# Off-by-one softmax attention and a squared-relu MLP on one core: relus and a copy moved to ScalarE, first-product steps moved between units, the last tile in two pieces

## The chip, the cores and the metric

The kernel runs on one core of one Trainium2 chip. A core has TensorE (PE, matrix products), VectorE (DVE), ScalarE (ACT), GpSimd (POOL) and SyncE (SP), each of which takes its instructions in order and waits for the others by semaphores. The metric is the device time of one execution in microseconds, as the median of several runs. The kernel before takes 412.63 us (three runs, 412.62 to 412.65).

## The reference

```python
batch, n_heads, seq, head_dim = (8, 12, 448, 64)        # q, k, v: float32
scale = 1.0 / np.sqrt(q.shape[-1])
scores = scale * np.matmul(q, k.transpose(0, 1, 3, 2))
m = np.max(scores, axis=-1, keepdims=True)
e = np.exp(scores - m)
attn = e / (np.sum(e, axis=-1, keepdims=True) + np.exp(-m) + 1e-09)
attn_out = np.matmul(attn, v)
# ...
x = np.ascontiguousarray(attn_out.transpose(0, 2, 1, 3)).reshape(B * S, H * D)   # 3584 x 768
h = x @ w_in                                             # 768 x 2048
r = np.maximum(h, 0.0)
g = r * r
out = (g @ w_out).astype(np.float32)                     # 2048 x 768
```

With the maximum taken out, attention is exp(s) divided by (sum of exp(s) + 1). The product with `w_in` is called the first product here, the one with `w_out` the second.

## The kernel before

Attention works in units: one pair of heads for some queries of one batch. Units 0 to 5 are the six pairs of batch 0 for its first 192 queries, units 6 to 11 the same pairs for the other 256, units 12 to 17 the pairs of batch 1 with all 448. From unit 18 on three units are taken together. A unit's scores come in two halves (`scores(u, et, 0)` and `scores(u, et, 1)`, here the first and second scores), each followed by exp on ScalarE. VectorE then adds the exps up (`add_chunks`), TensorE makes row sums from that with a matrix of ones, ScalarE makes the reciprocal by ln and exp, and VectorE normalises.

Beside the attention, the first product of the tokens already attended runs in small steps, to fill TensorE: `drain(ns)` takes steps from the queue `ins` until they have used up `ns`, and stops, also inside a tile. A tile of the first product covers two blocks of 128 hidden units in batch 0, has 12 steps there, and ends with relu and multiply. What is emitted where in these loops is also the order in which each engine gets it. Tiles in PSUM (`mp`, three buffers, before unit 18) are shared by the first product, the transposes and the row sums.

```python
    def transposes(b, pr):
        tp = mp_tile(FP16)
        for i, name in enumerate("qk"):
            for s in range(RUN):
                for h in range(2):
                    nc.tensor.transpose(tp[64 * h:64 * h + 64, i, P * s:P * s + P],
                                        naturals[name, b, pr][:, h, s, :], ident[0:P, 0:P])
        if b not in qks:
            qks[b] = qk_pool.tile([128, 3, COLS], FP16, name="qk")
        parts = (0, S // 2, S) if b == 0 and pr < 3 else (0, S)
        for x, y in zip(parts, parts[1:]):
            nc.vector.tensor_copy(qks[b][:, 0:2, pr * S + x:pr * S + y], tp[:, :, x:y])

    # ...
    def add_chunks(u, et, es, half, step):
        n = u[3]
        if n == S:
            e = et.rearrange("p (k x) -> p k x", k=RUN)
            if step < 2:
                nc.vector.tensor_add((es, half[:, 0:2 * S])[step], e[:, 2 * step], e[:, 2 * step + 1])
            else:
                nc.vector.tensor_add(es, es, half[:, 0:2 * S])
    # ...
    def row_sums(us, sums):

        n = us[0][3]
        m = n * len(us)
        zp = mp_tile()
        for j, (u, parts) in enumerate(zip(us, sums)):
            for x, es in enumerate(parts):
                total = es[:, 0:2 * n]
                if n < S:
                    total = total.rearrange("p (h n) -> p h n", h=2)
                for h in range(2):
                    nc.tensor.matmul(zp[64 * h:64 * h + 64, j * n:(j + 1) * n], ones, of_head(total, u, h),
                                     start=(x == 0), stop=(x == len(parts) - 1))
        rcp = z_pool.tile([128, 512], FP32, name="rcp")
        nc.scalar.activation(out=rcp[:, 0:m], in_=zp[:, 0:m], func=AF.Ln, bias=one_b)
        nc.scalar.activation(out=rcp[:, 0:m], in_=rcp[:, 0:m], func=AF.Exp, scale=-1.0)
        return rcp
    # ...
    def mp_tile(dtype=FP32):
        if joined[0] >= 0:
            joined[0] += 1
        pool, name = (x_psum, "xp") if joined[0] > 0 and joined[0] % 4 == 0 else (m_psum, "mp")
        return pool.tile([128, 512] if dtype == FP32 else [128, 2, 512], dtype, name=name)

    # ...
    def product(out_, lhsT, rhs, start, stop):

        if mode[0] == COLS2:
            for x in (0, 64):
                nc.tensor.matmul(out_[x:x + 64], lhsT[:, x:x + 64], rhs, start=start, stop=stop)
        else:
            nc.tensor.matmul(out_, lhsT, rhs, start=start, stop=stop)

    def relu_squared(hp, t0, n, f0, per):
        m = per * n
        rt = r_pool.tile([128, 512], FP16, name="rt")
        nc.vector.tensor_scalar(out=rt[:, 0:m], in0=hp[:, 0:m], scalar1=0.0, scalar2=None, op0=ALU.max)
        r = rt[:, 0:m].rearrange("p (j n) -> p j n", j=per)
        nc.vector.tensor_mul(gs[:, f0:f0 + per, t0 % RING:t0 % RING + n], r, r)

    def tile_in(t0, n, f0, per):

        xt, x0 = xts[t0 // S], t0 % S
        hp = mp_tile()
        for j in range(per):
            fb = f0 + j
            for dc in range(DCH):
                product(hp[:, j * n:(j + 1) * n], win[:, dc, fb * 128:(fb + 1) * 128],
                        xt[:, dc, x0:x0 + n], start=(dc == 0), stop=(dc == DCH - 1))
                if j < per - 1 or dc < DCH - 1:
                    yield n / 2.4
        relu_squared(hp, t0, n, f0, per)
        yield n / 2.4
    # ...
    def store(c, ot, n0, n1):
        end = c + 128
        while c < end:
            b = c // S
            step = RUN if b in ON_PE else 2
            rows = out[b * S:(b + 1) * S, n0:n1].rearrange("(p t) m -> t p m", t=step)
            t, p = c % S // (S // step), c % S % (S // step)
            m = min(S // step - p, end - c)
            o = c + 128 - end
            nc.sync.dma_start(out=rows[t, p:p + m, :], in_=ot[o:o + m, n0:n1])
            c += m

    # ...
    # end of tile_out(tok, n0, w): the second product of 128 tokens and w columns
        else:
            nc.scalar.activation(out=ot[:, n0:n0 + w], in_=op[:, 0:w], func=AF.Copy, scale=OUT_SCALE)
        # ...
        last = tok + 128 == NT
        if n0 + w == DM or last:
            store(tok, ot, n0 if last else 0, n0 + w)
        yield w / 2.4
    # ...
    def queue(t0, n):

        per = max(1, 512 // n)
        first = 0
        if t0 + n == FIRST:
            first = 2 * per
            ns = first * DCH * n / 2.4
            ins.append([ns, ns, tiles_in_early(n, 0, per, DCH - 2)])
        for f0 in range(first, NFFB, per):
            ns = per * DCH * n / 2.4
            ins.append([ns, ns, tile_in(t0, n, f0, per)])

    def complete(upto):

        while groups[0] + 128 <= upto:
            last = groups[0] + 128 == NT
            for n0, w in ((0, HALF), (HALF, 256), (HALF + 256, 128)) if last else ((0, HALF), (HALF, HALF)):
                ns = NFFB * w / 2.4
                outs.append([ns, ns, tile_out(groups[0], n0, w)])
            groups[0] += 128

    def left():
        return sum(t[0] for t in ins)

    def one(tiles):

        got = next(tiles[0][2])
        tiles[0][0] -= got
        if tiles[0][0] < 1.0:
            tiles.pop(0)
        return got

    def drain(ns):
        while ins and ns > 0:
            ns -= one(ins)

    def run(tiles, n=1):
        for _ in range(min(n, len(tiles))):
            for _ in tiles.pop(0)[2]:
                pass
    # ...
    FIRST = 192
    units = [(0, pr, 0, FIRST) for pr in range(NPAIR)] + [(0, pr, FIRST, S - FIRST) for pr in range(NPAIR)]
    units += [(b, pr, 0, S) for b in range(1, B) for pr in range(NPAIR)]
    NU = len(units)

    transpose_at = {pr - 1: [(0, pr)] for pr in range(1, NPAIR)}
    for i, at in ((10, (1, 0)), (11, (1, 1)), (11, (1, 2)), (13, (1, 3)), (14, (1, 4)), (15, (1, 5)), (16, (2, 0)),
                  (17, (2, 1)), (17, (2, 2))):
        transpose_at.setdefault(i, []).append(at)

    # ...
    for i in range(NPAIR, 2 * NPAIR):
        u, et, es, half = begin(i)
        two = units[i - 2:i] if i % 2 == 0 else None
        if i % 2 or i == NPAIR:
            xp = x_psum.tile([128, 512], FP32, name="xp")
        mode[0] = COLS2
        scores(u, et, 0)
        if i == NPAIR:
            sums(i - 1)
            values_of(i - 2, xp)
            values_of(i - 1, xp)
            rcp = sums_of(i - 2)
            normalise(two, xp, rcp)
            scores(u, et, 1)
            queue(0, FIRST)
            share[0] = left() / (NPAIR + 4)
        else:
            for at in transpose_at.get(i, ()):
                transposes(*at)
            drain(16 * FIRST / 2.4 if i == NPAIR + 1 else share[0] * 0.45)
            scores(u, et, 1)
            values_of(i - 1, xp)
            if two:
                rcp = sums_of(i - 2)
            drain(share[0] * 0.3)
        add_chunks(u, et, es, half, 1)
        if two and i > NPAIR:
            normalise(two, xp, rcp)
        add_chunks(u, et, es, half, 2)
        if i > NPAIR:
            drain(share[0] * 0.25)
        if i == NPAIR + 5:
            load_natural(2, 0, 3)
            for n0 in (0, HALF):
                for j in range(2):
                    load_wout(n0, j, 2)


    for i in range(2 * NPAIR, 3 * NPAIR):
        u, et, es, half = begin(i)
        prev = units[i - 1]
        first = i == 2 * NPAIR
        if not first:
            xp = x_psum.tile([128, 512], FP32, name="xp")
        mode[0] = COLS2
        scores(u, et, 0)
        for at in transpose_at.get(i, ()):
            transposes(*at)
        if i == 2 * NPAIR + 3:
            load_natural(2, 3, 6)
            load_v(2, 0, 6)
            stage(3)
        drain(share[0] * (1.2 if first else 0.45))
        scores(u, et, 1)
        if first:
            done = units[i - 2:i]
            values(prev, ets.pop(i - 1), xp, prev[3])
            rcp = row_sums(done, (ess.pop(i - 2)[0:1], ess.pop(i - 1)[0:1]))
        else:
            done = [prev]
            rcp = row_sums(done, (ess.pop(i - 1)[0:1],))
            values(prev, ets.pop(i - 1), xp)
        drain(share[0] * 0.15)
        for step in range(3):
            add_chunks(u, et, es, half, step)
            drain(share[0] * (0.15, 0.1, 0.15)[step])
        if i == 3 * NPAIR - 1:
            run(ins, len(ins))
            rcps[i] = row_sums([u], (ess.pop(i)[0:1],))
        normalise(done, xp, rcp)
        if first:
            queue(FIRST, S - FIRST)
            share[0] = left() / (NPAIR - 0.2)
    # ... units 18 to 47, then the last tokens: mode FULL, run(ins), run(outs)
```

Of the kernel before, what the change touches and what calls it, by code (L numbers as in the profile page):

```python
# [10 lines left out]
AF = mybir.ActivationFunctionType  # L11
ALU = mybir.AluOpType
# [3 lines left out]
def kernel(  # L16
# [9 lines left out]
    nc = tc.nc  # L26

    B, H, S, D = q.shape
    NT, DM = out.shape
    DF = moe_w_in.shape[1]  # L30
    NPAIR = H // 2
    DCH = DM // 128
    NFFB = DF // 128
# [4 lines left out]
    HALF = DM // 2  # L38
# [36 lines left out]
    whole, vns, qks, xts, naturals, stages = {}, {}, {}, {}, {}, {}  # L75
# [77 lines left out]
# [8 lines that stand above are left out]
            qks[b] = qk_pool.tile([128, 3, COLS], FP16, name="qk")  # L161
        parts = (0, S // 2, S) if b == 0 and pr < 3 else (0, S)
        for x, y in zip(parts, parts[1:]):
            nc.vector.tensor_copy(qks[b][:, 0:2, pr * S + x:pr * S + y], tp[:, :, x:y])  # L164

# [64 lines left out]
    def values(u, et, xp, o=0):  # L232
        b, pr, _, n = u
        for kk in range(RUN):
            for h in range(2):
                nc.tensor.matmul(xp[64 * h:64 * h + 64, o:o + n], vns[b][:, 2 * pr + h, kk, :],  # L236
                                 of_head(chunk(et, u, kk // 2, kk), u, h), start=(kk == 0), stop=(kk == RUN - 1))
# [18 lines that stand above are left out]
# [21 lines left out]

    FULL, COLS2, ROWS2 = range(3)
    mode = [FULL]
    ots = {}  # L280

    def product(out_, lhsT, rhs, start, stop):
# [7 lines left out]
    def relu_squared(hp, t0, n, f0, per):  # L290
        m = per * n
        rt = r_pool.tile([128, 512], FP16, name="rt")
        nc.vector.tensor_scalar(out=rt[:, 0:m], in0=hp[:, 0:m], scalar1=0.0, scalar2=None, op0=ALU.max)  # L293
        r = rt[:, 0:m].rearrange("p (j n) -> p j n", j=per)
        nc.vector.tensor_mul(gs[:, f0:f0 + per, t0 % RING:t0 % RING + n], r, r)  # L295

# [43 lines left out]
    def tile_out(tok, n0, w):  # L340

        if n0 == 0:
            ots[tok] = osb_pool.tile([128, DM], FP32, name="ot")
        ot = ots[tok]
        rows = mode[0] == ROWS2
        op = mp_tile()
        lo = mp_tile() if rows else None
        for fb in range(NFFB):
            g = gs[:, fb, tok % RING:tok % RING + 128]
            if rows:  # L350
                for x, o in ((0, op), (64, lo)):
                    nc.tensor.matmul(o[:, 0:w], g[x:x + 64], wout[x:x + 64, fb, n0:n0 + w],  # L352
                                     start=(fb == 0), stop=(fb == NFFB - 1))
            else:
                product(op[:, 0:w], g, wout[:, fb, n0:n0 + w], start=(fb == 0), stop=(fb == NFFB - 1))
            if fb < NFFB - 1:
                yield w / 2.4
        if rows:
            nc.vector.tensor_scalar(out=ot[:, n0:n0 + w], in0=op[:, 0:w], scalar1=OUT_SCALE, scalar2=None, op0=ALU.mult)
        else:  # L360
            nc.scalar.activation(out=ot[:, n0:n0 + w], in_=op[:, 0:w], func=AF.Copy, scale=OUT_SCALE)  # L361
        if rows:
            nc.vector.scalar_tensor_tensor(out=ot[:, n0:n0 + w], in0=lo[:, 0:w], scalar=OUT_SCALE,
                                           in1=ot[:, n0:n0 + w], op0=ALU.mult, op1=ALU.add)
# [4 lines that stand above are left out]
# [26 lines left out]
    ins, outs = [], []  # L395
    groups = [0]
# [13 lines left out]
    def complete(upto):  # L410

        while groups[0] + 128 <= upto:
            last = groups[0] + 128 == NT
            for n0, w in ((0, HALF), (HALF, 256), (HALF + 256, 128)) if last else ((0, HALF), (HALF, HALF)):
                ns = NFFB * w / 2.4
                outs.append([ns, ns, tile_out(groups[0], n0, w)])
            groups[0] += 128

    def left():
# [10 lines left out]
# [10 lines that stand above are left out]
# [14 lines left out]
    share = [0.0]  # L454
# [28 lines left out]
    def values_of(at, xp):  # L483
        values(units[at], ets.pop(at), xp, at % 2 * units[at][3])
# [38 lines left out]
# [16 lines that stand above are left out]
        else:  # L539
            for at in transpose_at.get(i, ()):  # L540
                transposes(*at)
            drain(16 * FIRST / 2.4 if i == NPAIR + 1 else share[0] * 0.45)
            scores(u, et, 1)
            values_of(i - 1, xp)
            if two:
                rcp = sums_of(i - 2)
            drain(share[0] * 0.3)
        add_chunks(u, et, es, half, 1)
        if two and i > NPAIR:
            normalise(two, xp, rcp)  # L550
        add_chunks(u, et, es, half, 2)
        if i > NPAIR:
            drain(share[0] * 0.25)
        if i == NPAIR + 5:
            load_natural(2, 0, 3)
            for n0 in (0, HALF):
# [25 lines that stand above are left out]
            done = [prev]  # L582
            rcp = row_sums(done, (ess.pop(i - 1)[0:1],))
            values(prev, ets.pop(i - 1), xp)
        drain(share[0] * 0.15)
        for step in range(3):
            add_chunks(u, et, es, half, step)
            drain(share[0] * (0.15, 0.1, 0.15)[step])
        if i == 3 * NPAIR - 1:
            run(ins, len(ins))  # L590
            rcps[i] = row_sums([u], (ess.pop(i)[0:1],))
        normalise(done, xp, rcp)
        if first:
            queue(FIRST, S - FIRST)
            share[0] = left() / (NPAIR - 0.2)
# [103 lines left out]
```

The softmax here doesn't subtract the row's maximum and nothing guards it: scores larger than these inputs give would overflow.

## Time and profile before

| | before |
|---|---|
| median time | 412.63 us |
| profiled span | 410.6 us |
| granted TensorE clock | 0.999 of full speed |
| VectorE relu of a first-product tile, 128x512 / 128x384 | 686 / 550 ns |
| VectorE multiply of it | 425 / 358 ns |
| VectorE copy of a transposed pair, 128x896 | 618 ns |
| VectorE addition of exps, 112x896 | some 620 ns |
| ScalarE exp of scores, 112x896 | 916 ns, one every 0.83 us |
| ScalarE ln, then exp, of row sums, 128x448 | 630, 577 ns |
| ScalarE table loads | 1, of 1.28 us |
| ScalarE output copy, 128x384 / 128x256 / 128x128 | 490 / 383 / 277 ns |

The durations are those of the groups of instructions, shapes kept apart; on VectorE and ScalarE the next instruction starts some 0.08 us before the recorded end of the one before it, if that one's result isn't needed. A timeline line gives start, duration, engine, source line and operation, output and input tile, shape and count, and in brackets how long the engine had been idle and what released it. The end of a matmul is modelled, so a matmul's bracket is a lower bound. The source lines that matter: L158 transposes, L164 their copy, L169 exp, L189 scores, L214 to L221 additions, L236 values, L250 row sums, L253 and L254 ln and exp, L262 and L265 normalise, L286 and L288 the products, L293 and L295 relu and multiply, L361 output copy, L337 store.

### The profile page before, as it was taken

The numbers are of one execution on the slowest core, as the hardware profiler recorded it, in microseconds if no ns is written. First come the engines' busy times: TensorE is split into PE (matmuls) and PEld (weight loads), VectorE is DVE, ScalarE is ACT, GpSimd is POOL, SyncE is SP. The second block draws the span as 40 slices with busy tenths as digits, with TensorE's granted clock in tenths as the row PEclk, the third lists the DMA queues.
The fourth block names the chain that finished last, engine by engine and source line by source line (L and its number), as shares of the span: only waits on it lengthen the run. The fifth ranks groups of instructions, "written<-read, shape, count | busy, mean of one in ns | idle before, by whom it ended". The sixth has DMA issues, their size and how long they took to land.

```text
span 410.6 us, 10685 instructions
## 1 busy us (share of the span) xinstructions
PE 401.0 (98%) x4715; PEld 259.0 (63%) x4715; DVE 289.8 (71%) x554; ACT 234.4 (57%) x312; POOL 36.3 (9%) x58
## 2 busy tenths in 40 slices
PE   7899998999999999999999999999999999999997
PEld 3577676755576666666566666667566665555664
DVE  3778896978976787777876788867876789186000
ACT  5998997667393745559383755739464663100111
POOL 7524030020000200001000030001000000000000
PEclk9999999999999999999999999999999999999999
DMA  9999999689114891499304992297102010010222
GB/s 203 197 198 197 203 202 219 127 132 219 60 42 107 135 219 25 98 183 182 100 2 114 168 179 64 77 188 124 41 2 69 11 41 2 38 40 0 78 77 78
DMA packets 75823, 45.58 MB, mean 111 GB/s; under 512 B 42560, under 2 KB 72000, under 8 KB 75456
## 3 DMA queue, kind: packets, MB, share of 16 engines
q0 software_dynamic: 28848, 22.16, 35.6%
q1 hardware_dynamic: 46208, 22.05, 23.1%
q8 instruction: 37, 0.61, 0.6%
q10 hardware_dynamic: 720, 0.69, 0.5%
q14 instruction: 10, 0.08, 0.1%
HBM read 45.69 MB, written 17.93 MB: 155 GB/s over the span
## 4 chain that ended last, share of the span: by engine, by line
PE 89%; ACT 4%; DVE 4%; DMA 1%; issue 1%
PE mp L286 24%; PE mp L352 17%; PE mp L288 11%; PE xp L286 8%; PE sp L201 6%; PE xp L352 5%; PE mp L236 5%; PE xp L288 3%; PE xp L236 3%; PE sp L189 3%; ACT et L169 3%; PE mp L250 2%; PE mp L158 1%; DMA et<-in_k_dram 1%; DVE qk L164 1%; ACT rcp L253 1%
## 5 line engine op out<-in xcount | busy, mean ns | idle before, releaser
L169 ACT ACTIVATE et<-sp 112x896 f16<-112x896 f32 (+2 forms) x144 | 125.2, 915 | 40.7 <-PE sp L201 30.6
L352 PE MATMUL mp<-wout,gs 64*128 64x384 f16 x896 | 115.2, 322 | 0.0
L286 PEld LDWEIGHTS <-win 128*64 128x64 f16 x1536 | 83.9, 110 | 45.6 <-issue 1.5
L286 PE MATMUL mp<-xt,win 128*64 128x448 f16 (+2 forms) x1200 | 107.0, 323 | 0.3 <-DVE qk L164 0.2
L293 DVE TENSOR_SCALAR rt<-mp 128x448 f16<-128x448 f32 (+2 forms) x96 | 59.7, 622 | 26.3 <-PE mp L286 13.8
L352 PEld LDWEIGHTS <-gs 64*128 64x128 f16 x1152 | 58.1, 94 | 21.1
L295 DVE TENSOR_TENSOR gs<-rt 128x448 f16<-128x448 f16 (+2 forms) x128 | 50.2, 392 | 4.4
L352 PE MATMUL xp<-wout,gs 64*128 64x384 f16 x256 | 53.1, 323 | 0.0
L253 ACT ACTIVATE rcp<-mp,one_b 128x448 f32<-128x448 f32 (+2 forms) x42 | 26.5, 630 | 41.9 <-PE mp L250 41.7
L361 ACT ACTIVATE ot<-mp 128x384 f32<-128x384 f32 (+1 forms) x16 | 7.6, 477 | 64.5 <-PE mp L288 48.2
L201 PE MATMUL sp<-qk 64*112 64x224 f16 x480 | 43.1, 258 | 0.0
L169 ACT ACTIVATE nn<-sp 112x896 f16<-112x896 f32 x48 | 41.7, 917 | 1.6
L201 PEld LDWEIGHTS <-qk 64*112 64x112 f16 x480 | 30.6, 128 | 14.2 <-issue 3.6
L286 PE MATMUL xp<-xt,win 128*64 128x448 f16 x336 | 36.5, 352 | 0.0
L288 PEld LDWEIGHTS <-gs 128*128 128x128 f16 x256 | 24.4, 98 | 15.1 <-issue 0.4
L236 PEld LDWEIGHTS <-vn 112*64 112x64 f16 x432 | 22.4, 109 | 15.4 <-issue 3.9
L288 PE MATMUL mp<-wout,gs 128*128 128x384 f16 (+1 forms) x192 | 30.3, 317 | 0.0
L214 DVE TENSOR_TENSOR es<-et 112x896 f16<-112x896 f16 x30 | 18.7, 623 | 15.8 <-ACT et L169 15.3
L254 ACT ACTIVATE rcp<-rcp 128x448 f32<-128x448 f32 (+2 forms) x48 | 27.7, 577 | 1.5
L189 PE MATMUL sp<-qk 64*112 64x448 f16 (+2 forms) x192 | 25.8, 320 | 1.4 <-ACT et L169 0.6
L216 DVE TENSOR_TENSOR es<-es,half 112x896 f16<-112x896 f16 x42 | 26.2, 623 | 1.0
L293 DVE TENSOR_SCALAR rt<-xp 128x448 f16<-128x448 f32 x32 | 19.9, 622 | 8.2 <-PE xp L286 6.7
(63 smaller groups left out, 340.0 us busy)
## 6 DMA issues: line engine op xcount, KB each, us to landing
vn<-in_v_dram POOLq DMA_DIRECT2D x7, 672.0 KB, 9.0
out_dram<-ot SPq DMA_DIRECT2D x9, 384.0 KB, 2.3
win<-in_moe_w_in_dram POOLq DMA_DIRECT2D x8, 384.0 KB, 14.2
wout<-in_moe_w_out_dram POOLq DMA_DIRECT2D x4, 768.0 KB, 18.0
stage_q<-in_q_dram POOLq DMA_DIRECT2D x4, 676.0 KB, 11.3
stage_k<-in_k_dram POOLq DMA_DIRECT2D x4, 676.0 KB, 14.7
out_dram<-ot SPq DMA_DIRECT2D x8, 288.0 KB, 9.0
out_dram<-ot SPq DMA_DIRECT2D x9, 192.0 KB, 2.7
```

The lines of the kernel that those rows point to most:

```text
L169: nc.scalar.activation(out=out_, in_=in_, func=AF.Exp, scale=scale)
L189: nc.tensor.matmul(sp[:, h, o:o + n], qk[r, 1, x + P * kk:x + P * kk + P], qk[r, 0, x + q0:x + q0 + n], start=True, stop=True)
L201: nc.tensor.matmul(sp[:, odd, h * (S // 2):(h + 1) * (S // 2)], qk[r, which, kx:kx + 2 * P - 1:2], qk[r, 0, x:x + S // 2], start=True, sto ...
L216: nc.vector.tensor_add(es, es, half[:, 0:2 * S])
L236: nc.tensor.matmul(xp[64 * h:64 * h + 64, o:o + n], vns[b][:, 2 * pr + h, kk, :], of_head(chunk(et, u, kk // 2, kk), u, h), start=(kk == 0 ...
L253: nc.scalar.activation(out=rcp[:, 0:m], in_=zp[:, 0:m], func=AF.Ln, bias=one_b)
L254: nc.scalar.activation(out=rcp[:, 0:m], in_=rcp[:, 0:m], func=AF.Exp, scale=-1.0)
L286: nc.tensor.matmul(out_[x:x + 64], lhsT[:, x:x + 64], rhs, start=start, stop=stop)
L288: nc.tensor.matmul(out_, lhsT, rhs, start=start, stop=stop)
L293: nc.vector.tensor_scalar(out=rt[:, 0:m], in0=hp[:, 0:m], scalar1=0.0, scalar2=None, op0=ALU.max)
L295: nc.vector.tensor_mul(gs[:, f0:f0 + per, t0 % RING:t0 % RING + n], r, r)
L352: nc.tensor.matmul(o[:, 0:w], g[x:x + 64], wout[x:x + 64, fb, n0:n0 + w], start=(fb == 0), stop=(fb == NFFB - 1))
```

## The change

It has three parts. In batch 1 the copy of the transposed pair 2 of batch 2, and the relus that end during the last unit (unit 17; a counter allows three), go from VectorE to ScalarE, so that VectorE comes sooner to the additions that the last row sums wait for. In units 7, 9 and 11 of batch 0 more first-product steps stand ahead of the second scores and fewer behind them, and in units 8 and 10 the row sums stand behind a drain instead of ahead of it, so that TensorE has work while ScalarE and VectorE catch up; unit 7's first drain keeps its length, so it does fewer steps in all. The last 128 tokens' second product is made in two pieces of 384 columns, as everywhere else, instead of 384, 256 and 128.

```diff
@@ -161,7 +161,11 @@
             qks[b] = qk_pool.tile([128, 3, COLS], FP16, name="qk")
         parts = (0, S // 2, S) if b == 0 and pr < 3 else (0, S)
         for x, y in zip(parts, parts[1:]):
-            nc.vector.tensor_copy(qks[b][:, 0:2, pr * S + x:pr * S + y], tp[:, :, x:y])
+            o, t = qks[b][:, 0:2, pr * S + x:pr * S + y], tp[:, :, x:y]
+            if (b, pr) == (2, 2):
+                nc.scalar.activation(out=o, in_=t, func=AF.Copy)
+            else:
+                nc.vector.tensor_copy(o, t)
 
 
 
@@ -277,6 +281,7 @@
 
     FULL, COLS2, ROWS2 = range(3)
     mode = [FULL]
+    relus = [0]
     ots = {}
 
     def product(out_, lhsT, rhs, start, stop):
@@ -290,7 +295,11 @@
     def relu_squared(hp, t0, n, f0, per):
         m = per * n
         rt = r_pool.tile([128, 512], FP16, name="rt")
-        nc.vector.tensor_scalar(out=rt[:, 0:m], in0=hp[:, 0:m], scalar1=0.0, scalar2=None, op0=ALU.max)
+        if relus[0]:
+            relus[0] -= 1
+            nc.scalar.activation(out=rt[:, 0:m], in_=hp[:, 0:m], func=AF.Relu)
+        else:
+            nc.vector.tensor_scalar(out=rt[:, 0:m], in0=hp[:, 0:m], scalar1=0.0, scalar2=None, op0=ALU.max)
         r = rt[:, 0:m].rearrange("p (j n) -> p j n", j=per)
         nc.vector.tensor_mul(gs[:, f0:f0 + per, t0 % RING:t0 % RING + n], r, r)
 
@@ -410,10 +419,9 @@
     def complete(upto):
 
         while groups[0] + 128 <= upto:
-            last = groups[0] + 128 == NT
-            for n0, w in ((0, HALF), (HALF, 256), (HALF + 256, 128)) if last else ((0, HALF), (HALF, HALF)):
-                ns = NFFB * w / 2.4
-                outs.append([ns, ns, tile_out(groups[0], n0, w)])
+            for n0 in (0, HALF):
+                ns = NFFB * HALF / 2.4
+                outs.append([ns, ns, tile_out(groups[0], n0, HALF)])
             groups[0] += 128
 
     def left():
@@ -539,18 +547,18 @@
         else:
             for at in transpose_at.get(i, ()):
                 transposes(*at)
-            drain(16 * FIRST / 2.4 if i == NPAIR + 1 else share[0] * 0.45)
+            drain(16 * FIRST / 2.4 if i == NPAIR + 1 else share[0] * (0.45 if two else 0.7))
             scores(u, et, 1)
             values_of(i - 1, xp)
+            drain(share[0] * (0.3 if two else 0.1))
             if two:
                 rcp = sums_of(i - 2)
-            drain(share[0] * 0.3)
         add_chunks(u, et, es, half, 1)
         if two and i > NPAIR:
             normalise(two, xp, rcp)
         add_chunks(u, et, es, half, 2)
         if i > NPAIR:
-            drain(share[0] * 0.25)
+            drain(share[0] * (0.25 if two else 0.2))
         if i == NPAIR + 5:
             load_natural(2, 0, 3)
             for n0 in (0, HALF):
@@ -582,12 +590,14 @@
             done = [prev]
             rcp = row_sums(done, (ess.pop(i - 1)[0:1],))
             values(prev, ets.pop(i - 1), xp)
+        relus[0] = 3 if i == 3 * NPAIR - 1 else 0
         drain(share[0] * 0.15)
         for step in range(3):
             add_chunks(u, et, es, half, step)
             drain(share[0] * (0.15, 0.1, 0.15)[step])
         if i == 3 * NPAIR - 1:
             run(ins, len(ins))
+            relus[0] = 0
             rcps[i] = row_sums([u], (ess.pop(i)[0:1],))
         normalise(done, xp, rcp)
         if first:
```

## The prediction

> **What bounds the kernel now.** I read the page's busy line first, then TensorE's timeline, then the chain of work that ended last, then the end of the run.
>
> ```profile
> PE 401.0 (98%) x4715; PEld 259.0 (63%) x4715; DVE 289.8 (71%) x554; ACT 234.4 (57%) x312; POOL 36.3 (9%) x58
> ```
>
> TensorE (PE) is busy through the span, and nothing else is near it. The change adds no first-product or attention matmuls, so only TensorE's pauses and the tail after its last matmul can move the time. TensorE's timeline (start, duration, what, and in brackets the idle time and its releaser) has these pauses from 25 us on:
>
> ```profile
> 25.96 0.41 PE L250 MATMUL mp<-es,ones 112*64 112x256 f16 x4 [0.20 <-DVE rt L293]
> 28.54 0.63 PE L236 MATMUL xp<-et,vn 112*64 112x256 f16 x8 [0.42 <-DVE xt L265]
> 38.08 0.40 PE L189 MATMUL sp<-qk 64*112 64x448 f16 x2 [0.19 <-ACT et L169]
> 42.56 0.40 PE L189 MATMUL sp<-qk 64*112 64x448 f16 x2 [0.41 <-ACT et L169]
> 52.78 0.38 PE L250 MATMUL mp<-es,ones 112*64 112x448 f16 x2 [0.20 <-DVE qk L164]
> 61.68 1.06 PE L286 MATMUL mp<-xt,win 128*64 128x256 f16 x16 [0.22 <-DVE qk L164]
> 67.21 0.38 PE L250 MATMUL mp<-es,ones 112*64 112x448 f16 x2 [1.13 <-DVE es L216]
> ```
>
> After 68 us I find no such pause, so whatever time is won or lost by the 67.21 line stays to the end. The third part aims at the last two lines, the second at the first four. How the 52.78 and 67.21 waits arise is in the chain (start, duration, what):
>
> ```profile
> 48.83 0.46 PE mp L286 x8
> 49.29 0.02 issue
> 49.31 0.70 DVE rt L293
> 50.02 0.02 issue
> 50.04 0.42 DVE gs L295
> 50.46 0.55 DVE half L214
> 51.01 0.02 issue
> 51.03 0.62 DVE es L216
> 51.66 0.54 DVE xt L262
> 52.19 0.54 DVE qk L164
> 52.74 0.04 issue
> 52.78 0.38 PE mp L250 x2
> ```
>
> A relu stands on VectorE (DVE) ahead of a unit's additions and waits for the last matmul of its first-product tile, though the additions could have run. Everything behind it is late, and after some 3.5 us TensorE waits for a copy. **A relu that VectorE meets before TensorE has its tile costs; one that it meets later is free.** That is what I look for in the changed order.
>
> **What the Trainium skill says.** "Trace Analysis", section "Identifying the Most-Contended Engine", says that matmul busy share is no good measure of headroom, and weight-load share is better. Here they are 98% and 63%: the small brackets above are what is left, and they understate the pauses (the 67.21 line starts 1.35 us after TensorE could have issued it, by the spacing of its neighbours). "ScalarE: Activation LUTs", section "Table sets: the hidden batching unit", has relu and copy in every table set, so no table reload should follow; the trace agrees for copy (one load, 1.28 us, in the whole run, with exp, ln and copy), and shows no ScalarE relu. Its "Rules for kernel authors" would keep relu on VectorE. By the trace a 128x512 activation without a pointer bias (L254) takes 631 ns, VectorE's relu of that size 686 ns. "DMA: Bandwidth & Descriptors", section "Anatomy of one DMA", has a fixed cost, mostly the write's receipt, plus a part by size. The trace agrees in kind: the last three stores of 192, 128 and 64 KB land 2.4, 1.7 and 1.5 us after issue.
>
> **Part 1, order in batch 0.** Call the first-product tiles T1 to T8 (192 tokens) and U1 to U8 (256), 12 steps each; a step is a pair of half-width matmuls, 80 or 107 ns. From the shares of 768 ns: unit 7 does 16+1+2 steps (before 16+3+3), units 9 and 11 do 7+1+2 (before 5+3+3), the others as many as before. So by unit 12's end 80 steps are done instead of 85.
>
> Walking TensorE with the trace's spacings (scores and switch 0.355 us, values 0.46, n steps 0.08n+0.13): the waits at 25.96 (relu of T1 ends at 25.91, after additions that wait for ScalarE) and 28.54 end where they did. From 28.54 fewer steps stand ahead of the next unit: unit 10 starts at 29.34 (29.59 before), unit 11 at 32.27 (32.51), unit 12 at 35.32 (35.87). Unit 12's exps start 0.55 earlier. ScalarE is then nearly back to back (0.83 each, ln and exp 1.25), so unit 13's last scores, at 42.56 before, come at about 42.07. That is 0.49 gained; but 4 to 5 steps (0.3 to 0.4) are only put off. Unit 14 starts at 44.67 (45.15).
>
> **Part 1, what it does later.** Steps done are shifted, so tiles finish at other places, and the built program's order on VectorE changes:
> - Unit 13: T8 no longer ends in the drain ahead of the second scores but in the one after the values. Its relu now stands ahead of unit 13's additions. T8 issues until 43.69, relu at 43.91 (0.22 later, as in the trace), then 384-wide relu 0.58, multiply 0.27, additions 0.54+0.66+0.54, normalise 0.54, and the copy ends 0.62 later, at 47.67. TensorE is ready for row sums 13 at 47.21 and starts at 47.73 (47.69 before): the gain is gone.
> - Unit 14: U2's relu moves behind one more addition; copy at 52.56, row sums at 52.62 (52.78 before). Unit 17 then starts at 59.67 (59.86).
> - Unit 16: U5 ends after the values, at 58.69, instead of in the earlier drain. Its relu, formerly at 57.50, waits until 58.91, and unit 16's additions stand behind it: 58.91 + relu 0.72 + multiply 0.35 + additions 0.54 + 0.66 + 0.54 + normalise 0.54 + copy 0.62 = 62.88. U7 needs the buffer of this copy. TensorE is there at 59.67 + scores 0.52 + transposes 0.81 + 4 steps 0.43 = 61.43 and waits until about 62.95. Before, U7 began at 61.68: 1.27 lost.
>
> **Part 2, ScalarE's copy and relus.** The copy (2,2) leaves VectorE 0.54 shorter, but the copy that U7 needs is (2,1), which stays and came first anyway. The counter is set to three, but only U7 and U8 finish before it is cleared: two relus move. VectorE's two multiplies stay, and U7's stands between unit 17's additions, so these now wait for ScalarE. ScalarE is in order too: U7's relu stands behind two exps, ln and exp of unit 17's stretch. From U7 at 62.95: 5 steps 0.66, second scores at 63.61, first of their exps 0.44 later at 64.05, two exps end 1.72 later at 65.77, ln 65.67 (it starts 0.1 before that end), exp +0.67, relu +0.52 = 66.86, end +0.63 = 67.49. Then VectorE's multiply 67.54, addition 67.89 to 68.53, and row sums 17 at about 68.6 against 67.21. TensorE would be ready at 67.2. So the old wait of 1.35 is replaced by about 1.4, and the shift at this point is +1.4.
>
> **Part 3, the last tile.** In the chain's end, 256 and 128 columns take 1.75 + 0.91 = 2.66, 384 columns 2.60: −0.06. The last activation takes 490 instead of 277 ns and starts some 85 instead of 37 ns after the last matmul, so the last store is issued 0.2 later. It carries 192 instead of 64 KB: 2.4 against 1.5 us to land, or 1.9 if I leave out a single straggling engine of the earlier 192 KB store, which shared its time with an instruction fetch. Sum +0.6 to +1.1, taken as +0.7. The lines (first timeline, then the store issues):
>
> ```profile
> 406.75 0.38 ACT L361 ACTIVATE ot<-xp 128x256 f32<-128x256 f32 x1 [1.21 <-PE xp L288]
> 407.65 0.28 ACT L361 ACTIVATE ot<-mp 128x128 f32<-128x128 f32 x1 [0.51 <-PE mp L288]
> ```
>
> ```profile
> out_dram<-ot SPq DMA_DIRECT2D x1, 192.0 KB, 2.4
> out_dram<-ot SPq DMA_DIRECT2D x1, 128.0 KB, 1.7
> out_dram<-ot SPq DMA_DIRECT2D x1, 64.0 KB, 1.5
> ```
>
> **Sum.** 412.63 + 1.4 + 0.7 = 414.7.
>
> **Rivals.** (a) It works as meant: the waits at 61.68 (0.44 by spacing) and 67.21 (1.35) vanish, the 0.49 stays, the tail costs 0.7: about 411. For it: VectorE's queue really is what both wait for. Against it: U7's multiply still holds the additions, and U5's relu comes late. (b) The two new VectorE waits are as before, and only the tail shows: about 413.3. That would be so if U5's relu were ready in time. (c) A table load around the relus, 1.28 us each: about 416; the one load in the trace speaks against it. (d) The last store is hidden by nothing, but the tail could land like the 128 KB one (1.7): 414.4.
>
> **Range and chances.** The sum hangs on two waits worked out step by step, each good to some 0.3 us, and on the tail, to 0.3. Rival (a) keeps a tenth of my belief. Range 413.2 to 415.6. Two per cent is 8.3 us, far more than any part here.
>
> **What would show it.** TensorE's timeline after: unit 13's last scores near 42.1; a wait of about 0.5 for a copy near 47.7; U7's start near 63 after 1.5 us of wait for the copy of (2,1); row sums 17 near 68.6, behind the multiply that waits for ScalarE's relu; two ScalarE relus, one ScalarE copy, one table load; the last store landing 1.9 us or more after issue. I am wrong if U7 starts before 61.7, or row sums 17 come before 67.2.

## The result, and the profile after

The changed kernel takes 414.39 us (414.17 to 414.94); the kernel before, on the same chip, 412.62 us. The ratio is 1.0045, with a 95% interval of 1.0028 to 1.0063: slower by 1.8 us, within 2%. The prediction was 414.7 us, in a range of 413.2 to 415.6.

The busy line of the page after says as little of this as the one before did. TensorE does less work by 16 matmuls (the last tile in two pieces) and is as busy as it was:

```profile
PE 401.4 (97%) x4699; PEld 257.9 (63%) x4699; DVE 288.0 (70%) x551; ACT 236.3 (57%) x314; POOL 36.8 (9%) x58
```

TensorE's timeline after, at the places shown of before from 40 us on (start, duration, what, and in brackets the idle time and its releaser; source lines have moved by some 4 to 9):

```profile
42.20 0.40 PE L193 MATMUL sp<-qk 64*112 64x448 f16 x2 [0.41 <-ACT et L173]
...
47.84 0.38 PE L254 MATMUL mp<-es,ones 112*64 112x448 f16 x2 [0.43 <-DVE qk L168]
...
52.65 0.38 PE L254 MATMUL mp<-es,ones 112*64 112x448 f16 x2
...
62.96 0.74 PE L291 MATMUL mp<-xt,win 128*64 128x256 f16 x10 [1.31 <-DVE qk L168]
...
68.46 0.38 PE L254 MATMUL mp<-es,ones 112*64 112x448 f16 x2 [1.10 <-DVE es L220]
```

The waits at 26 and 28.5 us, which are not shown again, are within 0.1 us of what they were (0.20 and 0.50 by their brackets). Three things are to be seen. The waits at 38.08 and 52.78 of before have gone. A new one stands at 47.84. The one at 61.68, which was 0.22 by its bracket, has become 1.31 at 62.96, and the one ahead of row sums 17 (those of unit 17), which the change was meant to remove, is still there at 68.46, in an order of VectorE that is new.

The chain of work that ended last, after (start, duration, what), ties the last two together:

```profile
58.59 0.35 PE mp L291 x6
...
58.96 0.70 DVE rt L302
...
62.38 0.54 DVE qk L168
...
62.96 0.74 PE mp L291 x10
...
64.07 0.21 ACT et L173
...
66.83 0.59 ACT rt L300
...
67.45 0.42 DVE gs L304
67.87 0.55 DVE es L220
...
68.46 0.40 PE mp L254 x2
```

U5's relu (L302) starts 20 ns after its tile's last matmul: VectorE had been standing there. Between it and the copy (L168) that lets U7 start lie, left out here, the multiply, unit 16's three additions and a normalisation, back to back. Then unit 17's second exps (L173), ScalarE's relu of U7 (L300), VectorE's multiply (L304) and the last addition (L220) follow each other to row sums 17.

At the end of the run, first ScalarE's timeline after and then the store issues of the last 9 us (operation, size, median time to land):

```profile
408.86 0.49 ACT L370 ACTIVATE ot<-xp 128x384 f32<-128x384 f32 x1 [2.06 <-PE xp L293]
```

```profile
out_dram<-ot SPq DMA_DIRECT2D x2, 192.0 KB, 1.9
```

One output copy of 384 columns ends the run, with one store of 192 KB behind it that takes 1.9 us to land.

All steps can be measured from one point. Executions differ by up to 0.5 us in when the first product starts (20.85 us before, 20.90 after, 21.3 in some runs below), so distances from its first matmul are compared:

| us after the first first-product matmul | before | predicted | after |
|---|---|---|---|
| unit 13's last scores | 21.71 | 21.22 | 21.30 |
| row sums 13 | 26.84 | 26.88 | 26.94 |
| row sums 14 | 31.93 | 31.77 | 31.75 |
| U7's first step | 40.83 | 42.10 | 42.07 |
| unit 17's second exps | 42.26 | 43.20 | 43.17 |
| ScalarE's relu of U7 | – | 46.01 | 45.93 |
| row sums 17 | 46.36 | 47.75 | 47.56 |
| first second-product matmul | 46.90 | – | 48.11 |

(The predicted column is the time in the prediction less the 20.85 us of before.) From the first second-product matmul to the end of the last matmul it is 339.86 us before and 339.82 after. From there to the end of the span it is 2.98 before and 3.59 after. So the difference is 1.21 us ahead of the second product, nothing for the next 340 us, and 0.61 us in the tail.

### The profile page after: what moved, and what is told of

Read it like the earlier page. It is cut to its first block, busy times and chain, and to the rows that moved or that the text cites. A ratio compares the mean times of both kernels' runs of the same rounds, so it can differ in the third digit from the quotient of the medians.

```text
span 412.4 us, 10647 instructions
## 1 busy us (share of the span) xinstructions
PE 401.4 (97%) x4699; PEld 257.9 (63%) x4699; DVE 288.0 (70%) x551; ACT 236.3 (57%) x314; POOL 36.8 (9%) x58
## 4 chain that ended last, share of the span: by engine, by line
PE 91%; DVE 4%; ACT 3%; issue 1%
PE mp L291 23%; PE mp L361 17%; PE mp L293 10%; PE xp L291 8%; PE sp L205 6%; PE xp L361 5%; PE mp L240 5%; PE xp L293 4%; PE xp L240 4%; PE sp L193 3%; ACT et L173 2%; PE mp L254 2%; PE mp L158 2%; PE mp L460 1%; DVE qk L168 1%
## 5 line engine op out<-in xcount | busy, mean ns | idle before, releaser
L173 ACT ACTIVATE et<-sp 112x896 f16<-112x896 f32 (+2 forms) x144 | 125.2, 916 | 40.5 <-PE sp L205 30.6
L302 DVE TENSOR_SCALAR rt<-mp 128x448 f16<-128x448 f32 (+2 forms) x94 | 58.3, 621 | 27.7 <-PE mp L291 15.1
L304 DVE TENSOR_TENSOR gs<-rt 128x448 f16<-128x448 f16 (+2 forms) x128 | 50.2, 392 | 5.3 <-ACT rt L300 1.0
L370 ACT ACTIVATE ot<-mp 128x384 f32<-128x384 f32 x15 | 7.4, 491 | 64.0 <-PE mp L293 47.7
L173 ACT ACTIVATE nn<-sp 112x896 f16<-112x896 f32 x48 | 41.7, 917 | 1.6
L293 PEld LDWEIGHTS <-gs 128*128 128x128 f16 x240 | 23.4, 98 | 15.8 <-issue 0.4
L293 PE MATMUL mp<-wout,gs 128*128 128x384 f16 x176 | 29.3, 326 | 0.0
L220 DVE TENSOR_TENSOR es<-es,half 112x896 f16<-112x896 f16 x42 | 26.2, 623 | 1.0
L302 DVE TENSOR_SCALAR rt<-xp 128x448 f16<-128x448 f32 x32 | 19.9, 622 | 8.2 <-PE xp L291 6.7
```

The costliest lines, as they stand in the source:

```text
L173: nc.scalar.activation(out=out_, in_=in_, func=AF.Exp, scale=scale)
```

## The experiments

The theory: the loss ahead of the second product comes from two queue positions. (1) Part 1 moves the last steps of U5 behind unit 16's values (the product with v), so VectorE meets its relu too early and U7 waits for a copy at the other end of VectorE's queue. (2) Part 2 puts U7's relu behind four ScalarE instructions, while its multiply stays on VectorE between the additions that row sums 17 need. The tail is a separate sum. The rivals: the loss belongs to the operations themselves (ScalarE's copy and relus being slow), or to the steps that part 1 does fewer of, or to one part alone.

### One part at a time

The first kernel is the kernel before with part 3 alone:

```diff
-            for n0, w in ((0, HALF), (HALF, 256), (HALF + 256, 128)) if last else ((0, HALF), (HALF, HALF)):
+            for n0 in (0, HALF):
```

> Only the last tile's second product in two pieces of 384 columns; all else as before. Theory (the tail is open to the end of the run): the last output copy is 0.2 us longer and the last store three times as large, so about +0.6 us, 413.2; TensorE's row sums 17 stay at 67.2. Rival (the tail hides behind what the end of the program waits for anyway): 412.6.

Measured: 413.21 us (412.89 to 414.54) against 412.60, ratio 1.0018 [1.0011, 1.0025]. The run ends as the kernel after does, with a 384-wide output copy of 0.49 us and a store of 192 KB that lands in 1.9 us. Up to the last matmul the trace is that of before (46.91 us to the first second-product matmul, 339.82 from there to the last); the tail is 3.58 us instead of 2.98. Part 3 costs 0.6 us, and no other part touches that.

The second kernel is the kernel before with part 1 alone, all relus and copies on VectorE:

```diff
-            drain(16 * FIRST / 2.4 if i == NPAIR + 1 else share[0] * 0.45)
+            drain(16 * FIRST / 2.4 if i == NPAIR + 1 else share[0] * (0.45 if two else 0.7))
             scores(u, et, 1)
             values_of(i - 1, xp)
+            drain(share[0] * (0.3 if two else 0.1))
             if two:
                 rcp = sums_of(i - 2)
-            drain(share[0] * 0.3)
# ...
-            drain(share[0] * 0.25)
+            drain(share[0] * (0.25 if two else 0.2))
```

> Only the moved first-product steps and row sums of batch 0; relus and copies all on VectorE, tail as before. Theory (a late relu of U5 blocks VectorE's queue): U7 starts near 62.9 as with the whole change, row sums 17 near 68.1, so +0.9, 413.5. Rival (the moved steps gain 0.4 us and the harm comes from ScalarE): 412.2.

Measured: 413.46 us (413.16 to 413.73), ratio 1.0022 [1.0013, 1.0032]. TensorE's timeline of this kernel:

```profile
63.10 0.74 PE L286 MATMUL mp<-xt,win 128*64 128x256 f16 x10 [1.31 <-DVE qk L164]
...
68.23 0.38 PE L250 MATMUL mp<-es,ones 112*64 112x448 f16 x2 [0.74 <-DVE es L216]
```

U7's wait is the whole 1.31 of the kernel after, with nothing on ScalarE. U7 is 1.25 us later than before, but does 5 steps ahead of the second scores instead of 8, so unit 17's second exps are 0.92 later, and row sums 17 are 0.85 later.

The third kernel is the kernel before with part 2 alone:

```diff
+            if (b, pr) == (2, 2):
+                nc.scalar.activation(out=o, in_=t, func=AF.Copy)
+            else:
+                nc.vector.tensor_copy(o, t)
# ...
+        if relus[0]:
+            relus[0] -= 1
+            nc.scalar.activation(out=rt[:, 0:m], in_=hp[:, 0:m], func=AF.Relu)
# ...
+        relus[0] = 3 if i == 3 * NPAIR - 1 else 0
```

> Only the copy (2,2) and the relus of U7 and U8 on ScalarE; steps and tail as before. Theory (U7's multiply stands ahead of unit 17's additions and waits for a relu behind exp, ln and exp on ScalarE): U7 starts at 61.7 as before, its relu on ScalarE begins near 65.9, row sums 17 near 68.2 instead of 67.2, so +1.0, 413.6. Rival (it works as meant, VectorE reaches the additions sooner): row sums 17 near 66.2, 411.6.

Measured: 413.57 us (413.39 to 415.01), ratio 1.0031 [1.0019, 1.0043]. The TensorE, ScalarE and VectorE timelines of this kernel, at unit 17's additions:

```profile
68.63 0.38 PE L254 MATMUL mp<-es,ones 112*64 112x448 f16 x2 [2.09 <-DVE es L220]
```

```profile
66.34 1.06 ACT L300 ACTIVATE rt<-mp 128x512 f16<-128x512 f32 x2
```

```profile
66.96 0.42 DVE L304 TENSOR_TENSOR gs<-rt 128x512 f16<-128x512 f16 x1 [3.27 <-ACT rt L300]
67.30 0.62 DVE L218 TENSOR_TENSOR half<-et 112x896 f16<-112x896 f16 x1
```

VectorE stands idle for 3.27 us at U7's multiply. The last exps of unit 17 end at 65.3, so the addition behind the multiply, which starts at 67.30, is held back by 2.0 us; it needs nothing from the relu. The relu takes about half a microsecond on ScalarE; what costs is its place, behind two exps, ln and exp, which fill ScalarE from 63.58 to the relu's start. U7's first step is where it was before (40.83 us after the first matmul), so the copy given to ScalarE neither helps nor harms U7. The purpose of part 2 turns into its opposite: row sums 17 are 0.95 us later.

The fourth kernel has parts 1 and 2 without part 3.

> The whole change but the tail, which stays in three pieces. Theory: both waits are in series but share the wait for unit 17's exps, so less than the sum of the two parts: +1.25, 413.9; row sums 17 near 68.4. Rival (the parts add up): +1.9, 414.5.

Measured: 413.93 us (413.75 to 414.21), ratio 1.0034 [1.0022, 1.0046]. It takes 48.10 us to the first second-product matmul, as in the kernel after (48.11), with the tail of before (2.96). The two parts do not add up: 0.85 and 0.95 alone, 1.20 together. Where the rest goes is in VectorE's order. From unit 17's second exps to row sums 17 it is 4.10 us before, 5.05 with part 2 alone and 4.39 with both. With part 1, U7 is further behind, and its multiply comes after the second of unit 17's three additions instead of ahead of it; one addition (0.66 us from start to start) then runs while VectorE would wait. 0.91 (the exps later) + 0.29 (4.39 − 4.10) = 1.20.

### The two queue positions, each mended alone

The kernel after, with U5 ended ahead of unit 16's second scores, so that its relu comes sooner. The share of steps of the two drains together stays as it is after the change:

```diff
-        drain(share[0] * (1.2 if first else 0.45))
+        drain(share[0] * (1.2 if first else 0.6 if i == 3 * NPAIR - 2 else 0.45))
# ...
-        drain(share[0] * 0.15)
+        drain(share[0] * (0.0 if i == 3 * NPAIR - 2 else 0.15))
```

> The whole change, but in unit 16 the three steps that end U5 stand ahead of the second scores instead of behind the values, so U5's relu is no longer waited for by VectorE. Theory: TensorE's wait for copy (2,1) before U7 shrinks from 1.5 to some 0.4 us and everything behind it comes 1.1 earlier: 413.3. Rival (U7's buffer, not U5's relu, is what holds: the wait stays near 1.5): 414.4.

Measured: 413.21 us (412.99 to 414.08) against 412.58, ratio 1.0016 [1.0009, 1.0022]. TensorE's timeline of this kernel:

```profile
62.01 0.74 PE L291 MATMUL mp<-xt,win 128*64 128x256 f16 x10 [0.21 <-DVE qk L168]
...
67.51 0.38 PE L254 MATMUL mp<-es,ones 112*64 112x448 f16 x2 [1.10 <-DVE es L220]
```

U7's wait falls from 1.31 to 0.21, and the wait of row sums 17 does not change: the two are separate. The time is 1.2 us less than after. In the traces it is 1.11 us to the first second-product matmul. Part 2 is still in this kernel, yet row sums 17 are only 0.10 us later than before, not 0.95 as with part 2 alone: unit 17's second exps are 0.19 earlier than before, because 5 steps of U7 stand ahead of the second scores instead of 8, and the stretch from them to row sums 17 is the 4.39 us of both parts together. So what part 2 costs hangs on where part 1 has put U7's end.

The kernel after, with all of unit 17's additions emitted ahead of its remaining drains, so that U7's multiply stands behind them:

```diff
+        if i == 3 * NPAIR - 1:
+            add_chunks(u, et, es, half, 0)
+            add_chunks(u, et, es, half, 1)
+            add_chunks(u, et, es, half, 2)
         for step in range(3):
-            add_chunks(u, et, es, half, step)
+            if i < 3 * NPAIR - 1:
+                add_chunks(u, et, es, half, step)
```

> The whole change, but unit 17's three additions stand ahead of its drains, so U7's multiply is behind them on VectorE; the relus stay on ScalarE. Theory: the wait ahead of row sums 17 goes from 1.3 us to about 0, then some 0.25 come back where the second product's buffer waits for U8's relu on ScalarE: 413.3. The wait before U7 stays at 1.5. Rival (the additions wait for unit 17's exps rather than for the multiply): wait of 0.7 or more left, 413.9.

Measured: 413.31 us (412.89 to 413.59), ratio 1.0015 [1.0007, 1.0023]. VectorE's timeline of this kernel:

```profile
66.69 0.63 DVE L220 TENSOR_TENSOR es<-es,half 112x896 f16<-112x896 f16 x1
67.65 0.42 DVE L304 TENSOR_TENSOR gs<-rt 128x512 f16<-128x512 f16 x1 [0.33 <-ACT rt L300]
```

VectorE goes on to the last addition and stands idle for the relu only afterwards. Row sums 17 start at 67.40, with no idle time ahead of them in the trace, though U7 still comes at 42.06 us after the first matmul. The relu on ScalarE is as late as it was; but nothing that TensorE needs at once stands behind its multiply now. Of the 1.27 us that row sums 17 gain, 0.3 is given back behind the first second-product matmul (340.12 us from there to the last matmul instead of 339.82): the second matmul stands 0.34 us behind the first, 0.05 after the end of U8's relu on ScalarE, where the two were 4 ns apart.

So the rivals fall. The operations themselves are the same in this kernel and in the kernel after, and the loss of part 2 is gone. The gain in time alone would not show that, since the same edit also takes a wait away from the kernel before (1.01 us, below). But row sums 17 are 0.94 us later here than in that kernel without any part of the change (46.29 against 45.35 us after the first matmul), and unit 17's second exps, which part 1 puts off, are 0.91 later by themselves: next to nothing is left for part 2. The steps put off are put off with U5 ended sooner as well, and the loss of part 1 is gone; and each part alone costs nearly as much as the other. Part 1's two edits (the steps, and the row sums of units 8 and 10 behind a drain) were not run apart.

The third queue position of the prediction, T8 in unit 13, is mended in the same way in the kernel after:

```diff
-        drain(share[0] * (1.2 if first else 0.45))
+        drain(share[0] * (1.2 if first else 0.63 if i == 2 * NPAIR + 1 else 0.45))
# ...
-        drain(share[0] * 0.15)
+        drain(share[0] * (0.0 if i == 2 * NPAIR + 1 else 0.15))
```

> The kernel after, with T8 ended ahead of unit 13's last scores (as T6 is ahead of unit 11's) and the drain behind those scores empty. Theory: T8's relu and normalisation then end before row sums 13 are due, so the wait ahead of them (0.69 us between neighbouring starts in the kernel after) falls to under 0.25; the wait of U7's first step (1.53) and that of row sums 17 (1.32) stay as they are; the time falls from 414.4 by 0.4 to 0.7, to about 413.8. Rival: the step order at T8 costs nothing that another wait does not take again (unit 13's last scores then stand later and unit 14's exps with them); then row sums 13 start on time and a later wait in units 14 to 17 grows by as much, 414.4.

Measured: 413.69 us (413.45 to 414.27) against 412.61, ratio 1.0024 [1.0015, 1.0034]. TensorE's timeline of this kernel:

```profile
42.51 0.40 PE L193 MATMUL sp<-qk 64*112 64x448 f16 x2 [0.19 <-ACT et L173]
...
47.32 0.38 PE L254 MATMUL mp<-es,ones 112*64 112x448 f16 x2
```

Unit 13's last scores come when they did after (21.30 us after the first matmul), with less idle time ahead of them, because the moved steps fill it. The wait ahead of row sums 13 has gone, U7's is unchanged (1.30 by its bracket), and the first second-product matmul is 0.64 us earlier. So T8's place took back what the earlier exps of unit 12 had won, as the prediction had it.

### A version that beats both

The additions ahead of the drains cure the old wait of 1.35 us without ScalarE too. The first kernel is the kernel before with that alone, the diff as above and everything else as before:

> The kernel before, with unit 17's additions ahead of its remaining first-product tiles and nothing else; all relus stay on VectorE and the last tile in three pieces. Theory: row sums 17 start at their spacing (wait 1.35 us in the kernel before, then under 0.4), but U7's and U8's relus now stand behind the additions and the normalisation of the unit before on VectorE, and the second product's second buffer waits for them by about half a microsecond: 412.1. Rival: the relus on VectorE leave time enough and ScalarE's share is not needed for the gain; then 411.6, as with U8's relu on ScalarE. Second rival: the additions first push U7's relu so late that first-product buffers come free too late and PE stops ahead of U8 for about 1 us: 412.6 or more.

Measured: 411.81 us (411.50 to 412.04) against 412.61, ratio 0.9977 [0.9967, 0.9988]. TensorE's timeline of this kernel:

```profile
66.18 0.38 PE L250 MATMUL mp<-es,ones 112*64 112x448 f16 x2
...
67.28 0.97 PE L352 MATMUL mp<-wout,gs 64*128 64x384 f16 x9 [0.19 <-ACT rcp L253]
```

Row sums 17 are 1.01 us earlier. The second product does wait for its second buffer by about the half microsecond expected (its second matmul stands 0.51 us behind the first, 0.06 in the kernel before), but the line names the ln of row sums 17, not a relu, and little of it lasts: from the first second-product matmul to the last it is 339.99 us, 0.13 more than before. The time lies between the 412.1 of the theory and the 411.6 of its first rival.

The second has in addition U8's relu on ScalarE, where the queue is empty by then (U7's relu stays on VectorE):

```diff
+        if on_act[0]:
+            nc.scalar.activation(out=rt[:, 0:m], in_=hp[:, 0:m], func=AF.Relu)
+        else:
+            nc.vector.tensor_scalar(out=rt[:, 0:m], in0=hp[:, 0:m], scalar1=0.0, scalar2=None, op0=ALU.max)
# ... in unit 17, round the rest of its first product, behind the additions and drains above
+            on_act[0] = True
             run(ins, len(ins))
+            on_act[0] = False
```

> The kernel before with two edits: unit 17's additions ahead of its drains, and U8's relu alone on ScalarE; steps and tail as before. Theory: the wait ahead of row sums 17 falls from 1.35 us to under 0.4, nothing else moves: -1.0, 411.6. Rival (the wait reappears as a wait of the second product for the relus of U7 and U8): 412.3 or more.

Measured: 411.61 us (411.48 to 412.28) against 412.58, ratio 0.9978 [0.9968, 0.9987]. U8's relu starts on ScalarE at 66.26, 30 ns behind the last matmul of its tile. The first second-product matmul stands at 45.95 us, as with the additions alone. The intervals of the two are the same, so a gain from ScalarE's relu is not shown; the 0.2 us shorter way through the second product (339.80 instead of 339.99) would be its size.

The last version puts all together: part 1's order in batch 0, T8 and U5 both ended ahead of their units' second scores, unit 17's additions first, U8's relu on ScalarE, and the last tile in three pieces:

```diff
-        drain(share[0] * (1.2 if first else 0.45))
+        fill = {2 * NPAIR + 1: 0.63, 3 * NPAIR - 2: 0.6}.get(i, 0.45)
+        drain(share[0] * (1.2 if first else fill))
# ... batch 0 as in part 1, additions first and U8's relu as above
-        drain(share[0] * 0.15)
+        drain(share[0] * (0.15 if fill == 0.45 else 0.0))
```

> As better, plus the moved steps of the change, but with T8 ended ahead of unit 13's second scores and U5 ahead of unit 16's. Theory (the moved steps gain their 0.4 us as long as no relu comes late): the 0.7 us wait at row sums 13 and the 1.5 before U7 fall below 0.5 each, 411.1. Rival (the moved steps gain nothing, the exps pace this stretch anyway): as better, 411.6.

Measured: 411.12 us (410.79 to 411.17), ratio 0.9961 [0.9949, 0.9974]. TensorE's timeline of this kernel:

```profile
61.42 0.74 PE L287 MATMUL mp<-xt,win 128*64 128x256 f16 x10 [0.21 <-DVE qk L164]
...
65.64 0.36 PE L250 MATMUL mp<-es,ones 112*64 112x448 f16 x2
```

The waits of the kernel after at 47.84 and 68.46 have gone and that at 62.96 is small, and the first second-product matmul is at 45.13 us, 1.77 earlier than before. 0.24 of it is given back by the last matmul (340.10 us instead of 339.86). The second product's second matmul stands 0.29 us behind the first here, 0.05 after the end of U8's relu on ScalarE (66.45), so that relu holds it up. This is the fastest of all that was run, by 1.5 us against the kernel before; the changed kernel was 1.8 us slower than the kernel before in a comparison of its own, so some 3.2 us lie between the two. That it beats the version ahead of it is not settled by the intervals, which overlap, though the single runs of the two, on one chip, do not (410.79 to 411.17 against 411.48 to 412.28).

## Why the prediction was right

- **What bounds the kernel.** Right: the whole difference is TensorE's pauses ahead of the second product (1.21 us) and the tail (0.61). The start and the 340 us from the second product on moved by 0.04 each.
- **Part 1, the gain in batch 0.** Right: unit 13's last scores came 0.41 us earlier (predicted 0.49), unit 12 started at 35.37 (35.32).
- **Part 1, T8.** Right: its relu starts behind VectorE's idle time at 44.04, and a wait of about 0.5 us appears ahead of row sums 13, which start at 47.84 (47.73). The run with T8 ended sooner got 0.7 us back.
- **Part 1, U5 and U7.** Right to 0.05 us in each line of the chain: relu at 58.96 (58.91), U7 at 62.96 (62.95). The run with U5 ended sooner got 1.2 us back.
- **Part 2.** Right in mechanism: two relus moved, not three; the copy given to ScalarE was not the one that TensorE waits for; the relu stood behind exps, ln and exp, and the additions behind its multiply. The term was some 0.2 too large: row sums 17 moved by 1.20 us, not 1.4. The relu takes 588 ns, not the 631 borrowed from an exp, and the steps from the second exps to row sums 17 took 4.39 us instead of 4.55.
- **Part 3.** Right: 0.61 us, taken as 0.7. The last store landed in 1.9 us, the lower of the two figures weighed. The store of the same size ahead of it took 1.9 us too in all five kernels with two pieces, where one store follows it, and 2.1 to 2.4 in all seven with three pieces, where two follow it; so the longer time went with its place.
- **Rivals.** (a) fell: both of VectorE's waits are there. (b) fell too: U7's wait is new; the 413.21 us of part 3 alone is what it would have been. (c) fell: one table load of 1283 ns in the whole run, though relu is now among ScalarE's functions, as the Trainium skill, "ScalarE: Activation LUTs", section "Table sets: the hidden batching unit", has it. (d), the tail at 1.7 us of landing, was near: 1.9.
- **The rule on relus.** Too strong as it stands in the prediction: a relu that VectorE meets early need not cost, if nothing that TensorE soon needs is held up behind it. In the kernel after, VectorE waits 0.60 us at this relu, and TensorE has no pause from 28.58 to 42.20:

```profile
31.95 0.56 DVE L302 TENSOR_SCALAR rt<-mp 128x384 f16<-128x384 f32 x1 [0.60 <-PE mp L291]
```

The two misses have the same sign and sum to 0.3 us: 1.4 + 0.7 predicted, 1.21 + 0.61 measured. What the prediction did not see is how far its parts depend on each other: it worked out both parts together in the built order, and so came near the total, but it did not say that part 1 alone and part 2 alone would cost 0.85 and 0.95.

## What to carry to other kernels

When work is moved to an idle engine, look for what stands ahead of it in that engine's queue and for what stands behind its consumer in the old one: the relu took 0.59 us on ScalarE, and its place held a ready addition on VectorE back by 2.0 us. When steps are moved between drains, list where each tile now ends, because the relu at its end can land ahead of ready work (0.7 us for T8, 1.2 for U5) and cancel what the move won. Parts that meet in one queue don't add up: 0.85 and 0.95 us alone were 1.20 together. Reordering the ready work alone, with no engine changed, gave 0.8 us here.

## What the runs showed of the hardware

The groups of instructions after, shapes kept apart (count, busy time, mean ns):

```profile
L302 DVE TENSOR_SCALAR rt<-mp 128x512 f16<-128x512 f32 x6 | 4.1, 684 | 1.2 <-PE mp L291 1.2
L300 ACT ACTIVATE rt<-mp 128x512 f16<-128x512 f32 x2 | 1.2, 588 | 0.0
```

ScalarE's relu of 128x512 float32 values in PSUM takes 588 ns, less than VectorE's 684. The Trainium skill, "ScalarE: Activation LUTs", section "What ACT_TABLE_LOAD costs", gives 186 ns plus 0.833 ns per element where scale and bias are immediate values; the estimate from it for 512 elements is 612 ns, and the trace agrees to 4%. Its "Rules for kernel authors" would keep relu on VectorE, which this shape does not bear out. For the copy of 128x896 16-bit values in PSUM it is the other way round: 921 ns on ScalarE against 618 on VectorE before.
